# Transposing the Q and K rows in 32x32 blocks on VectorE instead of on TensorE

## The chip, the cores and the metric

The kernel runs on one core of one Trainium2 chip. The metric is the device time of that core in microseconds (us), as the median of several runs; lower is better.

## The reference

A two-layer model, each layer an attention with a recurrent memory (A) and a gated mixer (B), both with a residual. The change lies in A:

```python
# x: 2048 x 512, 32 heads of 128, memory of 8 tokens, segments of 32 tokens
for s in range(n_seg):                          # 64 segments, one after the other
    h = concat([mem, x[s]])                     # 8 + 32 = 40 tokens
    q, k, v = h @ Wq, h @ Wk, h @ Wv            # for every head
    scores = q @ k.T * scale                    # 40 x 40 for each head
    scores = where(mask, scores, -1e9)
    p = softmax(scores)
    o = (p @ v) @ Wo
    mem = o[:8]                                 # the next segment's memory
    outs.append(o[8:])
```

The model is x + A(layernorm(x)), then x + B(layernorm(x)), and both once more with the same weights. The memory makes the 64 segments of an attention block a chain. There are two attention blocks, 128 segments in all.

## The kernel before

Each attention block (a_block) works through 16 groups of 128 tokens, each of 4 segments. All weights stay in SBUF. A segment's 40 tokens are split: hA holds 32 of them (8 of memory, which come late, and 24 of x), and the other 8 come from hB, the last 8 tokens of each segment of the group, gathered in 32 rows. So the projections of 32 tokens use 32-wide weights in four column groups of TensorE (tile_position (0, 32*cg)), each group with another 512 columns of W.

In order, a segment does:

- psm (L545): Q and K of hA, four quarters (j = 0, 2, 1, 3; j < 2 is Q, else K) of 16 matmuls of 512 columns. ScalarE copies each to SBUF as rows (L548): tokens of four column groups on the partitions.
- emit_T (L512): four TensorE transposes for each quarter, into PSUM (pst), and a copy to KQ (L516 on ScalarE, L518 on VectorE), where the head dimension lies on the partitions. KQ holds 80 columns a head: K of 32 tokens, K of 8, Q of 32, Q of 8. The parts of 8 come from prep_segment (L491, L492 on POOL), which takes them from KTB and QTB.
- emit_S (L565): scores, a matmul for each head, 64-wide weights and 40 columns, in two halves. Then the exponentials: ETm for the memory's queries (L567), ETt for the others (L586), and the mask (L587).
- emit_V (L530): values, 64 matmuls in eight pieces of 8, laid between the steps above. They are evacuated to vs (L536 ScalarE, L538 VectorE).
- The row sums for the memory's queries (psD L579, reciprocal L582, spread with L589), PT (L592), psOm (L597), uT (L600), pw (L610, the product with Wo of the 8 memory rows), pw_sb (L613, L614), pmT (L626) and a reduction into the next segment's hA (L628). This is the recurrence.
- The same for the other 32 queries: row sums (L602, L605), psRt (L619), PT (L622), psOt (L633), copies into oT4 (L643).

Work that does not belong to the recurrence fills the time: fill(2) at four places of a segment takes two steps each from generators. gen_block_ln normalizes and transposes the next group; gen_bpass (L424 to L440) computes Q and K of that group's hB: psb, a copy to rowsB (L433), four TensorE transposes (pstB, L437), a copy to KTB or QTB (L440), in twelve steps; gen_y (L449) multiplies the finished group by Wo, in eight steps (psy). The order of the instructions on an engine follows the code, though a scheduler may move an instruction that is ready ahead of one that is not.

PSUM has two pools of four banks: acc (psm, pst, psv, psb, pstB, pw, pmT, psy, pT) and att (psS, psD, psOm, psRt, psOt). KQ comes from a pool of three buffers.

Of the kernel before, what the change touches and what calls it, by code (L numbers as in the profile page):

```python
# [14 lines left out]
P = 128  # L15
DM = 512
# [311 lines left out]
def a_block(tc, c, xd, MV_in, MV_out, mem0, wqkv, Wo, S):  # L328
# [8 lines left out]
    with ExitStack() as ctx:  # L337
# [12 lines left out]

        m0 = rowp.tile([M, DM], BF16, name="m0", tag="rowsQK", bufs=4)
        nc.sync.dma_start(m0[:], mem0.rearrange("b m d -> (b m) d"))
# [59 lines left out]
        def gen_bpass(tb):  # L412
            bs = blk_state[tb]
            hB = bs["hB"]
            KTB = blkp.tile([P, H, 32], BF16, name="KTB")
            QTB = blkp.tile([P, H, 32], BF16, name="QTB")
            bs.update(KTB=KTB, QTB=QTB)
            pend = []
            for j in (0, 2, 1, 3):
                psb = acc.tile([P, 512], F32, name="psb")  # L420
                for kt in range(KT):
                    for cg in range(4):
                        W_sb, col0 = wcat(chunk_of(j, cg))
                        nc.tensor.matmul(psb[32 * cg:32 * cg + 32, :], lhsT=hB[:, kt, :], rhs=W_sb[:, kt, col0:col0 + 512],  # L424
                                         start=(kt == 0), stop=(kt == KT - 1), tile_position=(0, 32 * cg))
# [5 lines left out]
                if True:  # L431
                    rB = rowp.tile([P, 512], BF16, name="rowsB", bufs=2)
                    nc.vector.tensor_copy(rB[:], psb[:])  # L433
                    yield
                    pstB = acc.tile([P, 4, P], BF16, name="pstB")
                    for hh in range(4):
                        nc.tensor.transpose(pstB[:, hh, :], rB[:, hh * P:(hh + 1) * P], ident_bf[:])  # L437
# [48 lines left out]
        def prep_segment(s):  # L486
            tb, j4 = s // 4, s % 4
            bs = blk_state[tb]
            KQ = kqp.tile([P, H, 80], BF16, name="KQ")
            vs = vsp.tile([P, 16, DH], BF16, name="vs")  # L490
            nc.gpsimd.tensor_copy(KQ[:, :, 32:40], bs["KTB"][:, :, 8 * j4:8 * j4 + 8])  # L491
            nc.gpsimd.tensor_copy(KQ[:, :, 72:80], bs["QTB"][:, :, 8 * j4:8 * j4 + 8])  # L492
            seg_state[s] = dict(KQ=KQ, vs=vs)

        def segment(s):
            tb, j4 = s // 4, s % 4
            st = seg_state.pop(s)
            KQ, vs = st["KQ"], st["vs"]
            KQf = KQ[:].rearrange("p h c -> p (h c)")
            hA_cur, hA_nxt = hA[s % NHA], hA[(s + 1) % NHA]  # L500
# [3 lines left out]
            rows = {}  # L504
            pst_tiles = {}

            def emit_T(ti, j):
                if ti % 2 == 0:
                    pst_tiles[ti // 2] = acc.tile([P, 2, 4, P], BF16, name="pst")
                pst = pst_tiles[ti // 2][:, ti % 2]  # L510
                for hh in range(4):
                    nc.tensor.transpose(pst[:, hh, :], rows[j][:, hh * P:(hh + 1) * P], ident_bf[:])  # L512
                src = pst.rearrange("p hh (g2 c2 r) -> p hh g2 c2 r", g2=2, c2=2)
                dst = heads_view(KQ[:, :, 40:72] if j < 2 else KQ[:, :, 0:32], j % 2)
                if ti % 2 == 0:
                    nc.scalar.copy(dst, src)  # L516
                else:
                    nc.vector.tensor_copy(dst, src)  # L518

            vstate = {}  # L520

            def emit_V(c, half):
                if half == 0:
                    vstate[c] = acc.tile([P, 512], F32, name="psv")
                psv = vstate[c]
                for kt in range(2 * half, 2 * half + 2):
                    for cg in range(4):
                        g = cg // 2
                        col0 = 2048 * g + 512 * c
                        nc.tensor.matmul(psv[32 * cg:32 * cg + 32, :], lhsT=(hA_cur if cg % 2 == 0 else hB_cur)[:, kt, :],  # L530
                                         rhs=Wv_sb[:, kt, col0:col0 + 512],
                                         start=(kt == 0), stop=(kt == KT - 1), tile_position=(0, 32 * cg))
                if half == 1:
                    dstv = vs[:, 4 * c:4 * c + 4, :].rearrange("p h e -> p (h e)")
                    if c % 2 == 0:
                        nc.scalar.copy(dstv, psv[:])  # L536
                    else:
                        nc.vector.tensor_copy(dstv, psv[:])  # L538

            for ji, j in enumerate((0, 2, 1, 3)):  # L540
                psm = acc.tile([P, 512], F32, name="psm")
                for kt in range(KT):
                    for cg in range(4):
                        W_sb, col0 = wcat(chunk_of(j, cg))
                        nc.tensor.matmul(psm[32 * cg:32 * cg + 32, :], lhsT=hA_cur[:, kt, :], rhs=W_sb[:, kt, col0:col0 + 512],  # L545
                                         start=(kt == 0), stop=(kt == KT - 1), tile_position=(0, 32 * cg))
                r = rowp.tile([P, 512], BF16, name="rows", tag="rowsQK", bufs=4)
                nc.scalar.copy(r[:], psm[:])  # L548
# [5 lines left out]
                if ji == 2:  # L554
                    emit_T(1, 2)
            psS = [att.tile([P, 8, 40], F32, name="psS") for _ in range(2)]
            ETm = segp.tile([P, 16, 8], BF16, name="ETm")
            ETt = segp.tile([P, 16, 32], BF16, name="ETt")

            def emit_S(half):  # L560
                for hl8 in range(8):
                    for g in range(2):
                        hl = 8 * half + hl8
                        h = 16 * g + hl
                        nc.tensor.matmul(psS[half][64 * g:64 * g + 64, hl8, :], lhsT=KQf[:, 80 * h:80 * h + 64], rhs=KQ[:, h, 40:80],  # L565
                                         start=True, stop=True, tile_position=(0, 64 * g))
                nc.scalar.activation(out=ETm[:, 8 * half:8 * half + 8, :], in_=psS[half][:, :, 0:8], func=ACT.Exp, scale=scale)  # L567
# [17 lines left out]
            for half in range(2):  # L585
                nc.scalar.activation(out=ETt[:, 8 * half:8 * half + 8, :], in_=psS[half][:, :, 8:40], func=ACT.Exp, scale=scale)  # L586
            nc.gpsimd.tensor_tensor(out=ETt[:], in0=ETt[:], in1=maskT[:].unsqueeze(1).to_broadcast([P, 16, 32]), op=ALU.mult)  # L587
            for g in range(2):
# [10 lines left out]
            for g in range(2):  # L599
                nc.scalar.copy(uT_cur[:, 16 * g:16 * g + 16, 0:8], psOm[g][:])  # L600
            for cq in range(4):
                nc.tensor.matmul(psD[:, 2 + 2 * cq:4 + 2 * cq], lhsT=ETt[:, 4 * cq:4 * cq + 4, :].rearrange("p h q -> p (h q)"),  # L602
                                 rhs=ind[:, 0:2], start=True, stop=True)
            with nc.allow_low_precision(reason="softmax 1/denominator stored in bf16 (probabilities are bf16 anyway)"):
                nc.vector.reciprocal(out=Rc[:, 2:10], in_=psD[:, 2:10])  # L605
            fill(FILLU)
            pw = acc.tile([P, 512], F32, name="pw")
# [6 lines left out]
            nc.vector.tensor_copy(pw_sb[:, 256:512], pw[:, 256:512])  # L614
            fill(FILLU)
            psRt = att.tile([P, 512], F32, name="psRt")
            for cq in range(4):
# [23 lines left out]
            oT4 = blk_state[tb]["oT4"]  # L641
            for g in range(2):
                nc.vector.tensor_copy(oT4[:, 16 * g:16 * g + 16, 32 * j4:32 * j4 + 32], psOt[g][:])  # L643
            fill(FILLU)
# [54 lines left out]
```

## Time and profile before

| | us |
|---|---|
| median of 3 runs | 2994.6 (2994.12 to 3000.23) |
| the profiled execution | 2987.32 |
| its span | 2985.4 |
| PE busy | 2670.5 (89%) |
| DVE busy | 1057.1 (35%) |
| ACT busy | 908.3 (30%) |
| POOL busy | 325.4 (11%) |
| mean granted TensorE clock | 0.977 |

PE is TensorE's matmuls, PEld its weight loads, DVE VectorE, ACT ScalarE, POOL GpSimd. The chain is the work that ended last, followed back from the last instruction; its shares say where the span went. An instruction's line number, such as L545, is its line in the kernel. x16 is the number of instructions in a row. Where matmuls overlap, their own durations (a few hundred ns) say less than the time that a run of them takes in the chain.

### The profile page before, as it was taken

The page shows a single profiled execution, that of the slowest core. Times are in us where ns is not written, and L with a number is a line of the kernel's source. Part 1 is how long each engine was busy: PE and PEld are TensorE (multiplying, and loading weights), DVE is VectorE, ACT ScalarE, POOL GpSimd, SP SyncE. Part 2 cuts the span into 40 slices and gives each one's busy share as a digit, 9 for nine tenths or more (in the row PEclk, how much of TensorE's full clock was granted, in tenths as well). Part 3 has the DMA queues.
Part 4 walks back from the last instruction along what each step waited for, and adds up shares of the span by engine and source line. Part 5 has one row for each costly group of instructions (what it writes and reads, how often), then busy time and mean ns, then how long its engine had stood idle before and what let it go on. Part 6 is the DMA issues. An engine that isn't in the chain of part 4 may idle for free.

```text
span 2985.4 us, 94041 instructions
## 1 busy us (share of the span) xinstructions
PE 2670.5 (89%) x43154; PEld 1324.3 (44%) x43272; DVE 1057.1 (35%) x2582; ACT 908.3 (30%) x2114; POOL 325.4 (11%) x531
## 2 busy tenths in 40 slices
PE   0999999999999999983779999999999999999889
PEld 0444444444444444441554444444444444444456
DVE  3333333333333333341233333333333333333422
ACT  0333333333333333343003333333333333333430
POOL 1101110011001111000221110101001111111012
PEclk9999999999999999996898999999999999999999
DMA  8000000000000000027750000000000000000234
GB/s 316 2 10 9 9 9 9 9 9 9 9 9 9 9 9 9 6 97 134 155 169 2 9 9 9 9 9 9 9 9 9 10 9 9 9 9 5 97 89 110
DMA packets 105613, 107.80 MB, mean 36 GB/s; under 512 B 69776, under 2 KB 79360, under 8 KB 102144
## 3 DMA queue, kind: packets, MB, share of 16 engines
q1 hardware_dynamic: 79520, 46.88, 6.9%
q10 hardware_dynamic: 21728, 30.78, 3.0%
q0 software_dynamic: 3968, 24.12, 2.1%
q8 instruction: 338, 5.54, 0.7%
q14 instruction: 59, 0.48, 0.1%
HBM read 66.11 MB, written 18.87 MB: 28 GB/s over the span
## 4 chain that ended last, share of the span: by engine, by line
PE 82%; DVE 8%; issue 4%; DMA 3%; ACT 3%; POOL 0%; ACTq 0%; DVEq 0%; POOLq 0%; SPq 0%
PE psv L530 19%; PE psm L545 17%; PE pw L610 8%; PE psy L449 7%; PE pg L195 6%; PE pst L512 6%; PE psb L424 4%; PE psS L565 3%; DVE rowsB L433 2%; PE psOm L597 2%; PE pstB L437 2%; DVE vs L538 2%; PE pmT L626 2%; PE psOt L633 1%; DMA xb<-in_A_x_dram 1%
## 5 line engine op out<-in xcount | busy, mean ns | idle before, releaser
L530 PE MATMUL psv<-Wv_sb,hA 128*32 128x512 bf16 x4096 | 606.5, 383 | 0.0
L530 PE MATMUL psv<-Wv_sb,hBs 128*32 128x512 bf16 x4096 | 606.5, 383 | 0.0
L548 ACT CAST rows<-psm 128x512 bf16<-128x512 f32 x512 | 300.1, 586 | 881.2 <-PE psm L545 879.1
L518 DVE COPY KQ<-pst 128x512 bf16<-128x512 bf16 x256 | 108.7, 425 | 658.4 <-ACT vs L536 348.5
L587 POOL TENSOR_TENSOR ETt<-ETt,maskT 128x512 bf16<-128x512 bf16 x128 | 148.1, 1157 | 1282.0 <-ACT ETt L586 1281.8
L545 PE MATMUL psm<-Wq_sb,hA 128*32 128x512 bf16 x4096 | 274.3, 389 | 9.7 <-DVE hA L628 6.8
L545 PEld LDWEIGHTS <-hA 128*32 128x32 bf16 x8192 | 185.7, 97 | 205.9 <-issue 25.2
L545 PE MATMUL psm<-Wk_sb,hA 128*32 128x512 bf16 x4096 | 272.5, 387 | 0.0
L610 PE MATMUL pw<-Wo_sb,uT 128*32 128x512 bf16 x4096 | 249.5, 380 | 4.7 <-ACT uT L600 0.3
L195 PE MATMUL pg<-wspT,z2n 128*128 128x256 bf16 (+1 forms) x1536 | 176.6, 277 | 76.7 <-issue 76.7
L449 PE MATMUL psy<-Wo_sb,oT 128*128 128x512 bf16 x932 | 231.7, 380 | 8.5 <-issue 4.8
L538 DVE CAST vs<-psv 128x512 bf16<-128x512 f32 x256 | 177.1, 692 | 171.4 <-PE psv L530 171.4
L512 PEld LDWEIGHTS <-rows 128*128 128x128 bf16 x2048 | 116.3, 98 | 221.1 <-ACT KQ L516 107.0
L512 PE MATMUL pst<-ident_bf,rows 128*128 128x128 bf16 x2048 | 203.8, 222 | 0.9 <-ACT KQ L516 0.8
L195 PEld LDWEIGHTS <-z2n 128*128 128x128 bf16 (+1 forms) x1536 | 151.2, 100 | 101.9 <-issue 84.2
L536 ACT CAST vs<-psv 128x512 bf16<-128x512 f32 x256 | 150.1, 586 | 144.2 <-PE psv L530 144.2
L530 PEld LDWEIGHTS <-hA 128*32 128x32 bf16 x4096 | 155.0, 95 | 70.4
L530 PEld LDWEIGHTS <-hBs 128*32 128x32 bf16 x4096 | 154.9, 95 | 58.1
L643 DVE CAST oT<-psOt 128x512 bf16<-128x512 f32 x256 | 166.6, 683 | 6.4 <-PE psOt L633 6.2
L516 ACT COPY KQ<-pst 128x512 bf16<-128x512 bf16 x256 | 150.8, 589 | 22.3 <-PE pst L512 22.3
L610 PEld LDWEIGHTS <-uT 128*32 128x32 bf16 x4096 | 106.4, 96 | 113.0 <-ACT uT L600 16.1
L622 DVE TENSOR_TENSOR PT<-ETt,psRt 128x512 bf16<-128x512 bf16 x128 | 87.8, 686 | 145.4 <-PE psRt L619 139.6
(106 smaller groups left out, 2684.7 us busy)
## 6 DMA issues: line engine op xcount, KB each, us to landing
xs<-xd SPq DMA_DIRECT2D x48, 256.0 KB, 2.8
xs<-xd ACTq DMA_DIRECT2D x48, 256.0 KB, 4.9
xd<-xo SPq DMA_DIRECT2D x32, 256.0 KB, 2.0
Wq_sb<-in_A_Wq_dram POOLq DMA_DIRECT2D x6, 1024.0 KB, 32.7
Wk_sb<-in_A_Wk_dram POOLq DMA_DIRECT2D x6, 1024.0 KB, 41.1
Wv_sb<-in_A_Wv_dram POOLq DMA_DIRECT2D x6, 1024.0 KB, 31.6
Wo_sb<-in_A_Wo_dram ACTq DMA_DIRECT2D x4, 1024.0 KB, 14.8
Wo_sb<-in_A_Wo_dram POOLq DMA_DIRECT2D x4, 1024.0 KB, 20.3
```

The lines of the kernel that those rows point to most:

```text
L195: nc.tensor.matmul(pg[0:fsz, :], lhsT=z2n[:, st_i, f0:f0 + fsz], rhs=wspT[:, st_i, :], start=(st_i == 0), stop=(st_i == NT - 1))
L449: nc.tensor.matmul(psy[:, :], lhsT=bs["oT4"][:, h, :], rhs=Wo_sb[:, h, :], start=(h == 0), stop=(h == H - 1))
L512: nc.tensor.transpose(pst[:, hh, :], rows[j][:, hh * P:(hh + 1) * P], ident_bf[:])
L516: nc.scalar.copy(dst, src)
L530: nc.tensor.matmul(psv[32 * cg:32 * cg + 32, :], lhsT=(hA_cur if cg % 2 == 0 else hB_cur)[:, kt, :], rhs=Wv_sb[:, kt, col0:col0 + 512], st ...
L536: nc.scalar.copy(dstv, psv[:])
L538: nc.vector.tensor_copy(dstv, psv[:])
L545: nc.tensor.matmul(psm[32 * cg:32 * cg + 32, :], lhsT=hA_cur[:, kt, :], rhs=W_sb[:, kt, col0:col0 + 512], start=(kt == 0), stop=(kt == KT ...
L548: nc.scalar.copy(r[:], psm[:])
L587: nc.gpsimd.tensor_tensor(out=ETt[:], in0=ETt[:], in1=maskT[:].unsqueeze(1).to_broadcast([P, 16, 32]), op=ALU.mult)
L610: nc.tensor.matmul(pw[32 * cg:32 * cg + 32, :], lhsT=uT_cur[:, h, :], rhs=Wo_sb[:, h, :], start=(h < 4), stop=(h >= H - 4), tile_position= ...
L643: nc.vector.tensor_copy(oT4[:, 16 * g:16 * g + 16, 32 * j4:32 * j4 + 32], psOt[g][:])
```

## The change

- Q and K rows are transposed by VectorE, in 32x32 blocks from SBUF to SBUF, one instruction of 128x512 for each quarter, in emit_T and in gen_bpass. The TensorE transposes and the copies from PSUM are gone.
- So that blocks suffice, the four column groups of psm and psb no longer hold different heads but different 32-element parts of the same heads: qk_rhs reads W in runs of 32 elements, 128 elements apart.
- KQ is replaced by rings of three buffers KK and QQ, cleared once in each attention block. They hold, for each head, 32 columns for the 32 tokens and 32 columns for the 8 tokens, 24 of them zero. Scores are two matmuls for each head, with 32-wide weights and 64 columns, in four column groups.
- All vs copies go to ScalarE; of the two oT4 copies, one goes to ScalarE; the mask goes from POOL to VectorE.
- The row sums of the 32 queries and their reciprocal move behind pw and its filling. The filling place ahead of pw is removed: three fill(2) a segment instead of four. gen_bpass has eight steps instead of twelve.
- rowsQK has three buffers instead of four.

```diff
-        kqp = ctx.enter_context(tc.tile_pool(name="a_kq", bufs=3))
...
-        def heads_view(ap3, s2):
-            return ap3.rearrange("p (g2 s2 c2 hh) r -> p s2 hh g2 c2 r", g2=2, s2=2, c2=2)[:, s2]
+        def qk_rhs(j, kt, cg):
+            W_sb = Wq_sb if j < 2 else Wk_sb
+            return W_sb[:, kt, :].rearrange("p (g2 s2 i eb el) -> p s2 eb g2 i el", g2=2, s2=2, i=8, eb=4)[:, j % 2, cg]
...
+        NKQ = 3
+        KKr = [pers.tile([P, 2, 2, 16, 32], BF16, name=f"KK{i}") for i in range(NKQ)]
+        QQr = [pers.tile([P, 2, 2, 16, 32], BF16, name=f"QQ{i}") for i in range(NKQ)]
+        for t in KKr + QQr:
+            nc.gpsimd.memset(t[:], 0.0)
...
-                        W_sb, col0 = wcat(chunk_of(j, cg))
-                        nc.tensor.matmul(psb[32 * cg:32 * cg + 32, :], lhsT=hB[:, kt, :], rhs=W_sb[:, kt, col0:col0 + 512],
+                        nc.tensor.matmul(psb[32 * cg:32 * cg + 32, :], lhsT=hB[:, kt, :], rhs=qk_rhs(j, kt, cg),
...
-                    rB = rowp.tile([P, 512], BF16, name="rowsB", bufs=2)
-                    nc.vector.tensor_copy(rB[:], psb[:])
-                    yield
-                    pstB = acc.tile([P, 4, P], BF16, name="pstB")
-                    for hh in range(4):
-                        nc.tensor.transpose(pstB[:, hh, :], rB[:, hh * P:(hh + 1) * P], ident_bf[:])
-                    src = pstB[:].rearrange("p hh (g2 c2 r) -> p hh g2 c2 r", g2=2, c2=2)
-                    dst = heads_view((QTB if j < 2 else KTB)[:], j % 2)
-                    pend.append(lambda dst=dst, src=src: nc.vector.tensor_copy(dst, src))
-                    yield
+                rB = rowp.tile([P, 512], BF16, name="rowsB", bufs=2)
+                nc.vector.tensor_copy(rB[:], psb[:])
+                dst = (QTB if j < 2 else KTB)[:, j % 2].rearrange("p a b -> p (a b)")
+                pend.append(lambda dst=dst, rB=rB: nc.vector.transpose(out=dst, in_=rB[:]))
+                yield
...
             def emit_T(ti, j):
-                if ti % 2 == 0:
-                    pst_tiles[ti // 2] = acc.tile([P, 2, 4, P], BF16, name="pst")
-                pst = pst_tiles[ti // 2][:, ti % 2]
-                for hh in range(4):
-                    nc.tensor.transpose(pst[:, hh, :], rows[j][:, hh * P:(hh + 1) * P], ident_bf[:])
-                src = pst.rearrange("p hh (g2 c2 r) -> p hh g2 c2 r", g2=2, c2=2)
-                dst = heads_view(KQ[:, :, 40:72] if j < 2 else KQ[:, :, 0:32], j % 2)
-                if ti % 2 == 0:
-                    nc.scalar.copy(dst, src)
-                else:
-                    nc.vector.tensor_copy(dst, src)
+                dst = (QQ if j < 2 else KK)[:, 0, j % 2].rearrange("p a b -> p (a b)")
+                nc.vector.transpose(out=dst, in_=rows[j][:])
...
-                    if c % 2 == 0:
-                        nc.scalar.copy(dstv, psv[:])
-                    else:
-                        nc.vector.tensor_copy(dstv, psv[:])
+                    nc.scalar.copy(dstv, psv[:])
...
-            psS = [att.tile([P, 8, 40], F32, name="psS") for _ in range(2)]
+            psS = [att.tile([P, 8, 64], F32, name="psS") for _ in range(2)]
...
-                        nc.tensor.matmul(psS[half][64 * g:64 * g + 64, hl8, :], lhsT=KQf[:, 80 * h:80 * h + 64], rhs=KQ[:, h, 40:80],
-                                         start=True, stop=True, tile_position=(0, 64 * g))
+                        for part in range(2):
+                            nc.tensor.matmul(psS[half][64 * g + 32 * part:64 * g + 32 * part + 32, hl8, :],
+                                             lhsT=KK[:, part, half, 8 * g + hl8, :], rhs=QQ[:, :, half, 8 * g + hl8, :],
+                                             start=True, stop=True, tile_position=(0, 64 * g + 32 * part))
...
-            nc.gpsimd.tensor_tensor(out=ETt[:], in0=ETt[:], in1=maskT[:].unsqueeze(1).to_broadcast([P, 16, 32]), op=ALU.mult)
+            nc.vector.tensor_tensor(out=ETt[:], in0=ETt[:], in1=maskT[:].unsqueeze(1).to_broadcast([P, 16, 32]), op=ALU.mult)
...
-            for cq in range(4):
-                nc.tensor.matmul(psD[:, 2 + 2 * cq:4 + 2 * cq], ...   # row sums L602, reciprocal L605
-            fill(FILLU)
             pw = acc.tile([P, 512], F32, name="pw")
...
             fill(FILLU)
+            for cq in range(4):
+                nc.tensor.matmul(psD[:, 2 + 2 * cq:4 + 2 * cq], ...   # row sums, reciprocal
             psRt = att.tile([P, 512], F32, name="psRt")
...
-            for g in range(2):
-                nc.vector.tensor_copy(oT4[:, 16 * g:16 * g + 16, 32 * j4:32 * j4 + 32], psOt[g][:])
+            nc.scalar.copy(oT4[:, 0:16, 32 * j4:32 * j4 + 32], psOt[0][:])
+            nc.vector.tensor_copy(oT4[:, 16:32, 32 * j4:32 * j4 + 32], psOt[1][:])
```

More of the change, by code (lines that the diff above doesn't have):

```diff
@@ L349, in a_block @@
         att = _Tagged(ps_pool, "att", 4)
-        m0 = rowp.tile([M, DM], BF16, name="m0", tag="rowsQK", bufs=4)
+        m0 = rowp.tile([M, DM], BF16, name="m0", tag="rowsQK", bufs=3)
         nc.sync.dma_start(m0[:], mem0.rearrange("b m d -> (b m) d"))
@@ L414, in gen_bpass @@
             hB = bs["hB"]
-            KTB = blkp.tile([P, H, 32], BF16, name="KTB")
-            QTB = blkp.tile([P, H, 32], BF16, name="QTB")
+            KTB = blkp.tile([P, 2, 16, 32], BF16, name="KTB")
+            QTB = blkp.tile([P, 2, 16, 32], BF16, name="QTB")
             bs.update(KTB=KTB, QTB=QTB)
@@ L488, in prep_segment @@
             bs = blk_state[tb]
[L489 removed]
+            KK, QQ = KKr[s % NKQ], QQr[s % NKQ]
             vs = vsp.tile([P, 16, DH], BF16, name="vs")
[L491 to L493 removed]
+            nc.gpsimd.tensor_copy(KK[:, 1, :, :, 0:8], bs["KTB"][:, :, :, 8 * j4:8 * j4 + 8])
+            nc.gpsimd.tensor_copy(QQ[:, 1, :, :, 0:8], bs["QTB"][:, :, :, 8 * j4:8 * j4 + 8])
+            seg_state[s] = dict(KK=KK, QQ=QQ, vs=vs)
         def segment(s):
@@ L543, in segment @@
                     for cg in range(4):
-                        W_sb, col0 = wcat(chunk_of(j, cg))
-                        nc.tensor.matmul(psm[32 * cg:32 * cg + 32, :], lhsT=hA_cur[:, kt, :], rhs=W_sb[:, kt, col0:col0 + 512],
+                        nc.tensor.matmul(psm[32 * cg:32 * cg + 32, :], lhsT=hA_cur[:, kt, :], rhs=qk_rhs(j, kt, cg),
                                          start=(kt == 0), stop=(kt == KT - 1), tile_position=(0, 32 * cg))
-                r = rowp.tile([P, 512], BF16, name="rows", tag="rowsQK", bufs=4)
+                r = rowp.tile([P, 512], BF16, name="rows", tag="rowsQK", bufs=3)
                 nc.scalar.copy(r[:], psm[:])
@@ L600, in segment @@
                 nc.scalar.copy(uT_cur[:, 16 * g:16 * g + 16, 0:8], psOm[g][:])
-            for cq in range(4):
[L602 to L605, printed above, removed]
-            fill(FILLU)
             pw = acc.tile([P, 512], F32, name="pw")
@@ L615, in segment @@
             fill(FILLU)
+            for cq in range(4):
+                nc.tensor.matmul(psD[:, 2 + 2 * cq:4 + 2 * cq], lhsT=ETt[:, 4 * cq:4 * cq + 4, :].rearrange("p h q -> p (h q)"),
+                                 rhs=ind[:, 0:2], start=True, stop=True)
+            with nc.allow_low_precision(reason="softmax 1/denominator stored in bf16 (probabilities are bf16 anyway)"):
+                nc.vector.reciprocal(out=Rc[:, 2:10], in_=psD[:, 2:10])
             psRt = att.tile([P, 512], F32, name="psRt")
```

5 lines of the change are left out of this document (1 added, 4 removed).

## The prediction

> **What bounds the kernel now.** I read the page first: the share of each engine and the chain of work that ended last.
>
> ```profile
> span 2985.4 us, 94041 instructions
> PE 2670.5 (89%) x43154; PEld 1324.3 (44%) x43272; DVE 1057.1 (35%) x2582; ACT 908.3 (30%) x2114; POOL 325.4 (11%) x531
> ...
> PE 82%; DVE 8%; issue 4%; DMA 3%; ACT 3%; POOL 0%; ACTq 0%; DVEq 0%; POOLq 0%; SPq 0%
> PE psv L530 19%; PE psm L545 17%; PE pw L610 8%; PE psy L449 7%; PE pg L195 6%; PE pst L512 6%; PE psb L424 4%; PE psS L565 3%; DVE rowsB L433 2%; PE psOm L597 2%; PE pstB L437 2%; DVE vs L538 2%; PE pmT L626 2%; PE psOt L633 1%; DMA xb<-in_A_x_dram 1%
> ```
>
> TensorE holds 82% of the chain. Three of the listed pieces are what the change removes (pst 6%, pstB 2%) or stands around it (the rowsB wait on VectorE, 2%). So the question is what stands in the tensor queue of one segment, and where that queue waits. Next I took the busy time in the four segments of one group of 128 tokens, and in the group:
>
> ```profile
> 616.47:638.41 21.94, 21.54 (x320) 9.87 (x323) 5.39 (x12) 6.27 (x15) 1.87 (x3) 1.00 0.01 2
> 638.41:658.59 20.18, 18.05 (x340) 8.59 (x343) 10.96 (x30) 6.27 (x15) 1.16 (x1) 1.00 0.08 28
> 658.59:676.94 18.35, 17.73 (x332) 8.51 (x331) 6.64 (x16) 6.27 (x15) 1.86 (x3) 1.00 0.01 3
> 676.94:693.23 16.29, 15.50 (x292) 7.38 (x292) 5.22 (x13) 6.28 (x15) 2.65 (x6) 1.00 0.01 2
> 616.47:693.23 76.76, 72.82 (x1278) 34.35 (x1281) 28.21 (x70) 25.09 (x60) 7.54 (x12) 1.00 0.03 9
> ```
>
> The columns are the stretch, its length, then busy time of PE, PEld, DVE, ACT, POOL, and the granted clock (1.00). TensorE is busy 72.8 of 76.8 us; VectorE and ScalarE a third each. Two attention blocks of 16 groups give 32 groups, 32 x 76.76 = 2456 us of the span; the rest (the mixer blocks and the start) the change leaves as it is. Last, the chain in order of time through the fourth segment, which carries no filling work:
>
> ```profile
> 676.94 1.91 PE psm L545 x32
> 678.85 0.33 PE pst L512 x4
> ...
> 681.46 0.36 PE psS L565 x16
> ...
> 682.70 0.75 PE psv L530 x9
> ...
> 683.78 0.76 PE psv L530 x10
> ...
> 685.98 0.98 PE psv L530 x16
> ...
> 687.73 0.70 DVE vs L538
> ...
> 688.48 0.30 PE psOm L597 x8
> ...
> 688.82 0.28 ACT uT L600
> ...
> 689.14 1.91 PE pw L610 x32
> ...
> 691.33 0.70 DVE PT L622
> ...
> 692.88 0.30 DVE hA L628
> ```
>
> The columns are start, length, and the piece. Up to the last psv the chain never leaves TensorE: what is taken out of that queue shortens the segment by its full length. Behind it the chain goes through evacuations.
>
> **The change part by part.** The sum is made against the profiled execution, 2987.3 us (span 2985.4), which is 7.3 us under the median of the runs, 2994.6.
>
> Segment transposes. Four groups of four leave TensorE in each segment, 4 x 0.33 = 1.32 us, all on the chain. In their place VectorE gets four 32x32-block transposes of 128x512. The trace has none; the nearest rows are
>
> ```profile
> L548 ACT CAST rows<-psm 128x512 bf16<-128x512 f32 x512 | 300.1, 586 | 881.2 <-PE psm L545 879.1
> L587 POOL TENSOR_TENSOR ETt<-ETt,maskT 128x512 bf16<-128x512 bf16 x128 | 148.1, 1157 | 1282.0 <-ACT ETt L586 1281.8
> L516 ACT COPY KQ<-pst 128x512 bf16<-128x512 bf16 x256 | 150.8, 589 | 22.3 <-PE pst L512 22.3
> L622 DVE TENSOR_TENSOR PT<-ETt,psRt 128x512 bf16<-128x512 bf16 x128 | 87.8, 686 | 145.4 <-PE psRt L619 139.6
> ```
>
> I take 0.69 us, the VectorE row of as many elements; the ends are 0.59 (ScalarE's copies) and 1.16 us (POOL's row). Whether it hides is a matter of place:
>
> ```profile
> 601.38 0.59 ACT L548 CAST rows<-psm 128x512 bf16<-128x512 f32 x1 [4.64 <-PE psm L545]
> ...
> 602.24 0.59 ACT L548 CAST rows<-psm 128x512 bf16<-128x512 f32 x1 [0.28 <-PE psm L545]
> ...
> 604.85 0.59 ACT L548 CAST rows<-psm 128x512 bf16<-128x512 f32 x1 [0.72 <-PE psm L545]
> ```
>
> That segment began at 600.2. Row block 2 is in SBUF 2.6 us after the start, its transpose is done at 3.3; the first scores come after 64 psm matmuls, 2 x 1.91 = 3.8 us. Slack 0.5 us. Row block 3 is there at 4.6, less the two transposes (0.66) that no longer stand ahead of its matmuls, so at 4.0 to 4.6; its transpose ends by 5.3, and the second scores follow 24 psv matmuls at about 5.8. Slack 0.5 again. So the transposes cost nothing; without this cover they cost what rival B says. Three row buffers instead of four do no harm by this clock: the fourth row copy begins after the first transpose has ended.
>
> The value matmuls between the transposes come in odd pieces: 9 in 0.75 and 10 in 0.76, where 16 take 0.98 (0.061 each). Four of them work side by side in column groups, so a piece of 9 needs three turns. The excess is 0.35 us (1.51 - 19 x 0.061); with the transposes gone I take back 0.30, between 0 and 0.35.
>
> Scores. Sixteen matmuls of 40 columns with 64-wide weights (0.36 us, 22.5 ns each) become 32 of 64 columns with 32-wide weights, in four column groups, twice a segment. Ends: 0.36 us (the four groups side by side take it all up) and 32 x 22.5 ns = 0.72. Small matmuls issued as weight and product pairs stand in
>
> ```profile
> 636.15 0.50 PE psOt L633 x32
> ```
>
> 32 in 0.50 us. These are the nearest in number and width (32 columns), so I take 0.50: +0.14 a half, +0.28 a segment.
>
> The front of a segment therefore loses 1.32 + 0.30 - 0.28 = 1.34 us, x 128 = 171 us.
>
> The group's own projections (gen_bpass) and their filling. Same view of the chain, second and third segment:
>
> ```profile
> 652.52 0.89 PE psb L424 x16
> ...
> 653.44 0.70 DVE rowsB L433
> ...
> 655.13 0.59 PE pmT L626 x4
> ...
> 656.26 1.28 DVE oT L643 x2
> 657.54 0.61 DVE rowsB L433
> ...
> 670.55 0.76 PE psb L424 x11
> ...
> 673.04 0.33 PE pstB L437 x4
> ...
> 673.91 0.36 PE psRt L619 x8
> ...
> 674.97 0.70 DVE rowsB L433
> ```
>
> Here TensorE fills the time with psb and then waits for its own filling: rowsB has to leave PSUM before pstB can run, and in the second segment rowsB stands behind 1.28 us of oT. Second segment, from 652.52 to the next psm at 658.59: 6.07 us. With the transposes on VectorE, what is left there for TensorE is 32 psb (1.9), psRt (0.36), pmT (0.59) and psOt (0.50): 3.4 us, and nothing in it waits for rowsB. I take 2.6 off, since that tail is longer than the chain through pw_sb, pmT and the reduction. Third segment: from the end of pw, where pstB starts at 673.04, to 676.94 is 3.9 us, plus 16 psb ahead of pw, of which 11 took 0.76 (about 1.3 with the rest); afterwards 1.9 + 0.36 + 0.59 + 0.5 = 3.35, plus 0.36 for uT and 0.3 for vs, both uncovered: 5.2 - 4.0 = 1.2 off. The first segment loses the cover of uT (one of the four filling places is removed, the one that stood before pw): +0.36, less 0.2 for vs; +0.15. The fourth has the evacuation of vs by ScalarE (0.59 by the row of the same shape) instead of VectorE (0.70): -0.1. What remains of filling places, six units a segment, still carries the shorter list (eight units of psy, four of normalization, eight of psb) within the group. A group gains 2.6 + 1.2 - 0.15 + 0.1 = 3.75, x 32 = 120 us. Lower end 1.5 a group, 48 us, if what is late next (the reduction hA, 0.30, behind PT, 0.70, in VectorE's queue) takes its place.
>
> Moved and shifted work. VectorE loses two KQ copies, two vs copies and one oT half, and gains four transposes and the mask (0.69 us at most, by PT's row; POOL's took 1.157 and nobody on the chain waited for it): at or below 28 of 77 us busy. ScalarE swaps two KQ copies (0.589) for two vs copies (0.586) and gains one oT half of that price: about 7 of some 14 us. None is near to being the bound; their price is nothing as long as TensorE's queue is the longest. The row sums L602 and their reciprocal move behind pw. Without cover that is a reciprocal and psRt ahead of PT in the fourth segment; against it, the pw_sb copies now stand ahead of PT in VectorE's queue, and the reduction can come up to 0.8 us earlier. I take 0 for both, with -0.8 and +0.3 as ends (32 segments: -26 to +10 us).
>
> Once for each attention block, POOL clears six ring buffers of twice the elements of uT's memset:
>
> ```profile
> L380 POOL MEMSET uT<- 128x1024 bf16 x2 | 1.9, 949 | 58.9 <-DMA xd<-xf 58.8
> ...
> 73.88 0.61 PE pstB L437 x4
> ```
>
> 6 x 1.9 = 11.4 us ahead of the memsets that the first normalization waits for; 0 to 11 a block. I take 10 in all. The first group's projections, which run alone, lose three waits of 0.70 + 0.61: 4 us a block, 8 in all.
>
> Strided weights. psm and psb now read W as 16 runs of 32 elements, 128 apart, instead of 512 in a row. No matmul of the trace does that. Nearest: ScalarE's KQ copy writes runs of 32 at a pitch of 80 in 589 ns, its rows copy of the same size 586 in a row. So I take nothing; rival A has the other end. The Trainium skill, "SBUF — State Buffer", section "Door 1: The DMA port swizzle", says that reads keep full bandwidth if they hit a 16-byte line at least twice; a run of 32 bf16 does. No run here shows it for TensorE.
>
> **Sum.** 171 + 120 + 8 - 10 = 289 us. 2987.3 - 289 = 2698; with the 7.3 us of the median, 2706.
>
> **Rivals.**
> A, the other side: the strided weight reads stretch psm and psb. They are 128 + 32 times 3.8 us (64 matmuls, 2 x 1.91), 608 us in all. If they become 48% longer, the gain is gone; at twice the length the kernel takes 2706 + 608 = 3314 us. For it: every one of these matmuls changes, four column groups now read interleaved runs. Against it: ScalarE's row above. 7%.
>
> B, VectorE's transposes are late. At POOL's 1.16 us each the second ends at 1.8 (row block 0 is there, 601.97) + 2 x 1.16 = 4.1, 0.3 us after the scores want it. The fourth then ends at 6.4, where the second scores, themselves 0.3 late, want it at 6.1: another 0.3. 0.6 x 128 = 77 us back, 2783. It decides from about (3.8 - 1.8) / 2 = 1.0 us each. Against it: VectorE is idle most of a front. 10%. The Trainium skill, "VectorE: DVE Perf Modes", section "The three transpose paths", gives 311 ns for 128x128; four times that is an estimate of 1.24 us, and the time by the same steps would be about 2800. The trace has no such transpose.
>
> C, the scores are dear. At 22.5 ns each and with no odd pieces saved: +0.44 and +0.30 a segment, 95 us, 2801. For it: the same instruction with the same issue. Against it: 15.6 ns in psOt. 15%. The Trainium skill, "TensorE: Matmul & The Clock Gate", section "Wait — 56ns, not 53.3ns?", has a floor of about 25 ns from start to start for small matmuls; by it a half takes 0.80 us, and the sum would be 2706 + 0.60 x 128 = 2783. The psOt row is under that floor, which speaks against it here.
>
> D, the waits of the tails come back under another name (1.5 instead of 3.75 a group): 2778. 10%.
>
> E, more is gained: scores at 0.36 (-36), the reduction 0.8 us earlier (-26), memsets hidden (-10): 2634 and less. 10%.
>
> **How the numbers follow.** The forecast, 2706, has 48%, and reaches from 2650 to 2760. The range of 8 in 10 takes in B, C and D and most of E: 2620 to 2850. Slower needs A beyond 48%: 6%. Within 0.2%, which is about what a measurement of this kernel can tell from no change: 1%. Faster: 93%.
>
> **What would show it.** Group windows of about 67.5 us instead of 76.8; no pst and pstB rows; psS 32 in about 0.50 us; psv pieces of whole fours; vector transposes near 0.69 us; psm still 32 in 1.91 us (1.91 growing is A). A wait of the psS weight loads on VectorE of more than 0.1 us a half is B. Chains through rowsB gone from the second and third segments; if a wait of pw on uT, or of psm on hA, grows by more than 0.5 us a segment, that is D. The prediction is wrong if psm is longer, or if the fronts, psm to last psv, take over 9.8 us instead of the 10.8 of before.

## The result, and the profile after

The changed kernel takes 2541.2 us (median of 12 runs, 2521.2 to 2548.6) against 2991.2 us before (15 runs; the three that the prediction had gave 2994.6): a ratio of 0.8495, 95% interval 0.8471 to 0.8518, 450 us less. The forecast was 2706 with a range of 2620 to 2850. The sign was right, the size was not: 289 us less were forecast. The profiled execution has a span of 2538.3 us. One run of all those below, of the kernel with 64-wide scores, came at a granted clock of 0.936 where its fellows had 0.976 to 0.982, and is left out.

The page after: span, engines, and the chain by engine and by line.

```profile
span 2538.3 us, 96292 instructions
...
PE 2259.8 (89%) x44720; PEld 1210.5 (48%) x44808; DVE 1162.4 (46%) x2582; ACT 985.5 (39%) x2242; POOL 201.0 (8%) x415
...
PE 76%; DVE 7%; ACT 6%; DMA 5%; issue 4%; POOL 1%; SPq 0%; ACTq 0%; POOLq 0%; DVEq 0%
PE psv L517 17%; PE psm L528 16%; PE pw L589 10%; PE psy L447 9%; PE pg L195 7%; PE psb L428 4%; ACT vs L522 3%; PE psS L549 3%; PE pmT L610 2%; DMA xs<-xd 2%; PE psRt L603 2%; DVE rowsB L436 1%; DMA xb<-in_A_x_dram 1%; PE psOm L582 1%; PE py L206 1%
```

TensorE is busy for the same 89% of a shorter span. pst and pstB are gone from the chain, and rowsB is down from 2% to 1%; new in this list are ScalarE's vs copy (3%), a load, xs from xd (2%), and psRt (2%).

The windows of one group, the third, fourth, first and second segment, then the whole (columns as before: stretch, length, PE, PEld, DVE, ACT, POOL, the granted clock, and last the share and GB/s of the DMA engines):

```profile
617.23:631.61 14.38, 13.89 (x339) 7.23 (x332) 8.67 (x17) 6.62 (x16) 0.70 (x2) 1.00 0.01 3
631.61:644.88 13.27, 12.78 (x307) 6.60 (x307) 6.59 (x14) 6.76 (x17) 1.53 (x5) 1.00 0.01 2
644.88:664.36 19.48, 19.14 (x341) 9.62 (x347) 5.96 (x12) 6.66 (x16) 0.74 (x2) 1.00 0.01 3
664.36:681.59 17.23, 14.72 (x347) 7.47 (x347) 10.26 (x28) 7.46 (x17) 0.00 (x0) 1.00 0.10 33
617.23:681.59 64.36, 60.53 (x1330) 30.93 (x1328) 31.48 (x69) 27.51 (x64) 2.97 (x8) 1.00 0.04 11
```

76.76 us have become 64.36. The granted clock is 1.00 in both. This group is a long one, since its second segment waits for a load (below): by the median, a group went from 76.7 to 63.0 us.

Call front what lies between the start of a segment's psm and the end of its last psv, and tail what follows up to the next psm. Added up from the records of the two traces, the 128 fronts are 326 us shorter and the 126 tails within the two attention blocks 114, of 447 us by which the span is shorter; all the rest differs by 7. The chain through the fourth segment (631.61 to 644.88) is the counterpart of the one the prediction shows:

```profile
631.61 3.64 PE psm L528 x64
635.25 0.26 PE psS L549 x32
635.50 1.31 PE psv L517 x24
636.82 0.28 PE psS L549 x32
637.10 0.87 PE psv L517 x16
637.97 0.11 PE psD L564
638.08 0.98 PE psv L517 x16
...
639.24 0.57 PE psv L517 x8
639.83 0.59 ACT vs L522
...
640.73 0.34 PE psRt L603 x8
...
641.08 1.94 PE pw L589 x32
643.04 0.38 ACT pw_sb L592
...
644.54 0.30 DVE hA L612
```

And the pieces of the same segment before that the prediction did not show:

```profile
679.18 0.98 PE psm L545 x16
...
680.49 0.98 PE psm L545 x16
681.83 0.55 PE psv L530 x8
...
684.90 0.97 PE psv L530 x13
...
687.13 0.57 PE psv L530 x8
```

This front took 10.77 us and takes 8.20 (631.61 to 639.81): 2.57 us, where 1.34 was forecast. The reader can add it up: the transposes 1.32; psm 3.87 (1.91 + 0.98 + 0.98) to 3.64, 0.23; psS 0.72 to 0.54, 0.18; psv 4.58 (0.55 + 0.75 + 0.76 + 0.97 + 0.98 + 0.57) to 3.73, 0.85.

At the start of an attention block two forecast terms meet, the memsets and the first group's projections, which run alone. Chain at the start of the first block, before and then after:

```profile
71.18 1.93 PE psb L424 x16
...
103.72 1.91 PE psm L545 x32
```

```profile
65.89 5.85 POOL KK L382 x3
...
79.00 3.50 PE psb L428 x32
...
97.84 3.64 PE psm L528 x64
```

From the first psb to the second segment's psm: 32.5 us before, 18.8 after. The ring memsets delay that psb by 7.8 us, in this block alone; in the second they end while a transfer of 13.6 us (xd from xo) is still under way. The projections, from that psb to the first psm, take 8 us less in the first block and 7 in the second.

### The profile page after: what moved, and what is told of

It is laid out like the page before. It is cut to its first block, busy times and chain, and to the rows that moved or that the text cites. A ratio compares the mean times of both kernels' runs of the same rounds, so it can differ in the third digit from the quotient of the medians.

```text
span 2538.3 us, 96292 instructions
## 1 busy us (share of the span) xinstructions
PE 2259.8 (89%) x44720; PEld 1210.5 (48%) x44808; DVE 1162.4 (46%) x2582; ACT 985.5 (39%) x2242; POOL 201.0 (8%) x415
## 4 chain that ended last, share of the span: by engine, by line
PE 76%; DVE 7%; ACT 6%; DMA 5%; issue 4%; POOL 1%; SPq 0%; ACTq 0%; POOLq 0%; DVEq 0%
PE psv L517 17%; PE psm L528 16%; PE pw L589 10%; PE psy L447 9%; PE pg L195 7%; PE psb L428 4%; ACT vs L522 3%; PE psS L549 3%; PE pmT L610 2%; DMA xs<-xd 2%; PE psRt L603 2%; DVE rowsB L436 1%; DMA xb<-in_A_x_dram 1%; PE psOm L582 1%; PE py L206 1%
## 5 line engine op out<-in xcount | busy, mean ns | idle before, releaser
L517 PE MATMUL psv<-Wv_sb,hBs 128*32 128x512 bf16 x4096 | 535.3, 381 | 0.0
L517 PE MATMUL psv<-Wv_sb,hA 128*32 128x512 bf16 x4096 | 534.7, 381 | 0.0
L522 ACT CAST vs<-psv 128x512 bf16<-128x512 f32 x512 | 299.6, 585 | 154.1 <-PE psv L517 137.2
L528 PEld LDWEIGHTS <-hA 128*32 128x32 bf16 x8192 | 209.9, 97 | 240.4 <-DVE hA L612 25.4
L528 PE MATMUL psm<-Wq_sb,hA 128*32 128x512 bf16 x4096 | 266.3, 380 | 18.8 <-DVE hA L612 18.8
L517 PEld LDWEIGHTS <-hA 128*32 128x32 bf16 x4096 | 180.5, 95 | 107.7
L505 DVE STREAM_TRANSPOSE QQ<-rows 128x512 bf16<-128x512 bf16 x256 | 181.4, 709 | 79.3 <-ACT rows L531 72.0
L626 ACT CAST oT<-psOt 128x512 bf16<-128x512 f32 x128 | 74.9, 585 | 365.2 <-PE psy L447 230.2
L505 DVE STREAM_TRANSPOSE KK<-rows 128x512 bf16<-128x512 bf16 x256 | 181.6, 709 | 29.3 <-ACT rows L531 24.7
L447 PEld LDWEIGHTS <-oT 128*128 128x128 bf16 x1024 | 95.1, 98 | 120.6 <-issue 12.7
L490 POOL COPY QQ<-QTB 128x256 bf16<-128x256 bf16 x128 | 49.6, 402 | 1272.2 <-DVE QTB L438 1222.1
L549 PEld LDWEIGHTS <-KK 128*32 128x32 bf16 x8192 | 89.7, 97 | 90.0 <-DVE KK L505 86.6
```

The source lines that it names most:

```text
L447: nc.tensor.matmul(psy[:, :], lhsT=bs["oT4"][:, h, :], rhs=Wo_sb[:, h, :], start=(h == 0), stop=(h == H - 1))
L505: nc.vector.transpose(out=dst, in_=rows[j][:])
L549: nc.tensor.matmul(psS[half][64 * g + 32 * part:64 * g + 32 * part + 32, hl8, :], lhsT=KK[:, part, half, 8 * g + hl8, :], rhs=QQ[:, :, hal ...
L626: nc.scalar.copy(oT4[:, 0:16, 32 * j4:32 * j4 + 32], psOt[0][:])
```

## The experiments

Theory M, formed on the trace after: what the forecast missed is the price of changing TensorE's tiling. A matmul whose weights are 128 or 64 wide, among matmuls with 32-wide weights in four column groups, costs about 0.11 us on the way in and again on the way out, besides its own work, as if the array ran empty each time. Before, a front changed eight times for transposes and four for 64-wide scores. The trace after carries the reading: 16 psv take 0.87 us behind psS, which is 32 wide, and 0.98 behind psD, which is not. Rival I: each instruction has its price. All changes below are against the changed kernel's 2541 us, and the ratios in brackets against the kernel before. The stretch between the two attention blocks, which these edits hardly touch, takes 247 to 282 us in the traces (270 in the one after the change); so the sums of fronts and tails from the traces are given beside the medians.

**A full-width matmul at four places, and its control.**

```diff
                 psm = acc.tile([P, 512], F32, name="psm")
+                if ji >= 2:
+                    nc.tensor.matmul(psm[:, 0:2], lhsT=ident_bf[:], rhs=ident_bf[:, 0:2], start=True, stop=True)
...
                     vstate[c] = acc.tile([P, 512], F32, name="psv")
+                    if c < 2:
+                        nc.tensor.matmul(vstate[c][:, 0:2], lhsT=ident_bf[:], rhs=ident_bf[:, 0:2], start=True, stop=True)
# control: the same, with
+  nc.tensor.matmul(psm[0:32, 0:2], lhsT=ident_bf[:, 0:32], rhs=ident_bf[:, 0:2], start=True, stop=True, tile_position=(0, 0))
```

> The changed kernel with one matmul of 2 columns and full 128-wide weights put in at four places of each segment: ahead of the third and fourth psm quarter and of the first two psv tiles. Its output is overwritten. Theory M: each place costs a change of the array's tiling forth and back, about 0.22 us, four a segment, 128 segments: 113 us slower (80 to 130). Rival (what cost time before was the transposes' own streaming, and a full-array matmul costs only its columns): under 10 us.

> The control to the run with a full-width matmul at four places: the same four places, 2 columns, but 32-wide weights in column group 0, the tiling that stands around it. Theory M: no change of tiling, at most a short turn of the array for each, 0.02 to 0.06 us, 10 to 30 us slower. If any inserted instruction costs the 0.22 us, it is as slow as the other, about 113 us.

Full width: 2631.6 us, 90 slower (ratio 0.8789, 0.8747 to 0.8831). Narrow: 2543.7, 3 slower (0.8507, 0.8473 to 0.8541). The chains, full width first (L529 and L513 are the inserted matmuls), then the control:

```profile
658.11 1.91 PE psm L532 x32
660.02 0.11 PE psm L529
660.13 0.98 PE psm L532 x16
...
661.21 0.98 PE psm L532 x16
```

```profile
648.50 3.66 PE psm L532 x61
```

One matmul of two columns stands 0.11 us in the chain and makes the 16 behind it take 0.98 instead of 0.87; psm goes from 3.64 to 4.09 us for two of them. The same instruction with 32-wide weights leaves 3.66. So it is not the instruction. Nor is it the width alone, by a row of the trace after:

```profile
656.64 3.19 PE psy L447 x14
```

psy has 128-wide weights behind 128-wide ones, and 512 columns take 0.228 us each there, about as much as a turn, four tiled matmuls of 512 columns side by side (0.87 / 4 = 0.218). The price of theory M is shown, at 0.22 us for a visit of another width. That the array runs empty meanwhile is a reading; no run here looks inside. The front grew by 0.83 us (658.11 to 667.14), which x 128 would be 106 us. The fronts of the whole trace are 92 us longer and the tails unchanged: the front of the second segment grew by 0.41 only, as it was waiting for something else (below).

**Scores 64 wide again.**

```diff
-                        for part in range(2):
-                            nc.tensor.matmul(psS[half][64 * g + 32 * part:64 * g + 32 * part + 32, hl8, :],
-                                             lhsT=KK[:, part, half, 8 * g + hl8, :], ..., tile_position=(0, 64 * g + 32 * part))
+                        i0 = min(8 * g + hl8, 14)
+                        nc.tensor.matmul(psS[half][64 * g:64 * g + 64, hl8, :],
+                                         lhsT=KK[:, 0, half, i0:i0 + 2, :].rearrange("p h c -> p (h c)"), ..., tile_position=(0, 64 * g))
```

> The changed kernel, but the scores are 16 matmuls a half with 64-wide weights in two column groups, as before the change, instead of 32 with 32-wide weights in four. The weights are two heads' K side by side, so the rows for the 8 late tokens hold other values; this is for time alone. Theory M (TensorE pays about 0.11 us whenever the width of the column tiles changes: a piece of 16 psv takes 0.87 us behind the 32-wide psS and 0.98 behind psD): psS then starts and ends with such a change, 0.26 grows to about 0.33 and the psv piece behind it by 0.11, 0.18 a half, 256 halves, 46 us slower (35 to 60). Theory I (a price for each instruction): half the matmuls, up to 0.13 a half less, 33 us faster.

2573.2 us, the median of three runs from 2564.5 to 2597.6, 32 slower (0.8618, 0.8558 to 0.8679). M said 46, and 35 to 60 as a range. The three runs are too far apart to tell these, but the fronts of the trace (of the run of 2597.6 us) are 45 us longer and its tails unchanged.

```profile
662.59 0.37 PE psS L549 x16
662.96 1.41 PE psv L517 x24
```

Half as many matmuls take 0.37 instead of 0.26 us, and the psv behind them 1.41 instead of 1.31. Rival I had this faster.

**Every score matmul twice.** `for part in range(2)` becomes `for part in (0, 1, 0, 1)`.

> The changed kernel with every score matmul issued twice (64 instead of 32 a half, same result). If four 32-wide matmuls stream side by side, a further four cost their 64 columns only, about 27 ns: +0.21 to 0.26 a half, 55 to 66 us slower. If each small matmul has a price of about 16 ns (the 0.50 us for 32 psOt on which the prediction rested): +0.5 a half, 131 us slower.

2632.4 us, 91 slower (0.8798, 0.8747 to 0.8850): between the two numbers. The chain of a half, and TensorE's waits (the trace is of a run of 2618.5 us):

```profile
663.68 0.51 PE psS L549 x47
```

```profile
PE psS L549 <- issue: 18.4, 18, 1.5
...
PE psv L517 <- issue: 12.3, 18, 1.2
```

32 further matmuls (the chain shows 47 of the 64) add 0.24 us a half, 7.5 ns each, 61 us in all. The 16 ns an instruction of the prediction is refuted for these matmuls. The fronts of this trace are 99 us longer in all; another 31 us of that are 18 pauses in the scores and 18 behind them, up to 1.5 us, for which the view shows no releaser, and some 8 are not assigned. The kernel after has no such pause. The trace's DMA records say what they are likely to be. The instruction queue q8 moves blocks of 16 KB, 414 here and 350 after the change: 64 more, for 16,384 more matmuls and weight loads. The records show 37 such pauses, 30.8 us, and each ends 1.2 to 1.6 us after a block has landed, though one lands only every 4.8 us (median). So TensorE most likely waited for its own instructions; no run took that cause away.

**The segment's transposes back on TensorE**, with W read in rows for psm; the new KK and QQ stay (the diff is shortened).

```diff
+                for hh in range(4):
+                    nc.tensor.transpose(pst[:, hh, :], rows[j][:, hh * P:(hh + 1) * P], ident_bf[:])
+                dst = (QQ if j < 2 else KK)[:, 0, j % 2].rearrange("p (g2 c2 hh) r -> p hh g2 c2 r", g2=2, c2=2)
+                (nc.scalar.copy if ti % 2 == 0 else nc.vector.tensor_copy)(dst, src)   # src: pst by head
-                nc.vector.transpose(out=dst, in_=rows[j][:])
```

> The changed kernel with the segment's transposes alone put back: psm reads W in rows of 512 and four groups of four TensorE transposes go to pst and from there to the new KK and QQ by ScalarE and VectorE, as before; all else is as changed. Theory M (transposes at 0.33, three pieces of psm instead of one, psv in odd pieces with a tiling change at each): 1.32 + 0.22 + 0.85 = 2.4 us a segment, 306 us slower. By the prediction's terms (1.32 + 0.30): 207 us slower.

2802.3 us, 261 slower (0.9370, 0.9335 to 0.9405), nearer to M's 306 than to the 207 of the prediction's terms.

```profile
672.96 0.33 PE pst L513 x4
...
675.83 0.45 PE psv L531 x8
676.27 0.33 PE pst L513 x4
676.60 0.75 PE psv L531 x9
677.35 0.33 PE pst L513 x4
677.68 0.76 PE psv L531 x10
```

The first psv piece, behind the 32-wide psS, takes 0.45 us for 8; the pieces behind transposes are 9 and 10 and take 0.75 and 0.76, three turns and a change of tiling (3 x 0.218 + 0.11 = 0.76). A front is 10.34 us here (634.12 to 644.46) against 8.20: 2.14, x 128 = 274; the fronts of the whole trace are 261 us longer, the tails unchanged. M's 306 held the changes around 64-wide scores too, which this run does not have. This one edit is more than half of the change's gain.

**The transposes of gen_bpass back on TensorE**, psb reading W in rows, with the filling place and the order of the row sums before the change, which its twelve steps need.

> The changed kernel with the transposes of gen_bpass put back on TensorE (twelve steps instead of eight), and with the row sums and the fourth filling place back ahead of pw, which the twelve steps need. By the prediction's tails 3.8 us a group, 32 groups, and the start: 100 to 130 us slower. If the waits on rowsB are covered now that VectorE has fewer copies from PSUM: the pstB groups alone, 4 x 0.4 us a group, 51 us slower.

2604.4 us, 63 slower than the changed kernel (0.8709, 0.8664 to 0.8753), but it holds the next experiment's order, which by itself is 26 us faster. Against that one it is 89 us slower. By the traces 81 us of this lie in the tails, 2.6 a group, and 8 at the start of the first block.

**The row sums and the filling place back ahead of pw.**

```diff
+            for cq in range(4):
+                nc.tensor.matmul(psD[:, 2 + 2 * cq:4 + 2 * cq], ...)
+            ... nc.vector.reciprocal(out=Rc[:, 2:10], in_=psD[:, 2:10])
+            fill(FILLU)
             pw = acc.tile([P, 512], F32, name="pw")
```

> The changed kernel with the row sums L602, their reciprocal and the filling place put back ahead of pw. The prediction put this move at nothing but the cover of uT (0.36 us in one or two of four segments): between 20 us faster and 10 slower. If the move is part of why the tails came out shorter: over 20 us slower.

2514.9 us, 26 faster (0.8412, 0.8380 to 0.8444), a little over the end of what was expected; the tails of its trace are 29 us shorter. The row sums themselves did not move: the changed kernel has them behind pw in its code, but its trace has them (L596) and psRt (L603) ahead of pw in all 128 segments, so the scheduler had put them there. What this run gives back is the filling place. TensorE's waits for the next group's tokens, after and in this run:

```profile
PE psb L428 <- DVE hB L414: 38.0, 30, 10.4
```

```profile
PE psb L428 <- DVE hB L414: 10.2, 2, 8.6
```

With the filling place gone, the next group's token transposes stand behind pw, and psb waits for nine VectorE copies out of them. With it, they stand between parts of psOm and are done under pw. Removing the filling place costs time.

**Copies and mask on their old engines** (vs by halves on VectorE, both oT4 copies on VectorE, the mask on POOL).

> The changed kernel with the copies and the mask where they were: two of four vs copies and both oT4 copies on VectorE, the mask on POOL. Expected: the last vs copy 0.70 instead of 0.59 ahead of psOm, 0.11 a segment, 14 us slower; if VectorE's longer queue makes the transposes late (its four take 0.71 each), 0.3 to 0.5 a segment more, 50 to 80 us slower.

2607.9 us, 67 slower (0.8715, 0.8676 to 0.8753). The number fell where late transposes were expected, but hardly for that reason: a front is 8.02 us long in this run (643.88 to 651.90) as after the change (617.23 to 625.25), and all fronts together are 10 us longer. It is the tails, 80 us longer together, while the stretch between the blocks is 23 shorter in this trace:

```profile
670.33 0.19 PE psRt L606
670.61 0.70 DVE PT L609
...
672.16 0.30 DVE hA L615
```

Here one psRt is left behind pw, PT follows it, and hA waits behind PT in VectorE's queue: 2.18 us from pw to the next psm, against 1.86 (643.02 to 644.88) after the change, where PT runs under pw. With 0.11 for vs, that is 0.43 us a segment, 55 of the 80 us; the rest lies in the second and third segments of the groups (their tails are 1.13 and 0.61 us longer) and is not assigned.

**W in rows again** (Q and K hold other columns).

> The changed kernel with psm and psb reading W in rows of 512 elements instead of 16 runs of 32; Q and K then hold other columns, so this is for time alone. The prediction's rival A (strided reads stretch these matmuls) would make it faster by what they are stretched; the trace has 64 psm in 3.64 us, 57 ns each, no longer than before. Expected: no difference, within 10 us.

2541.3 us, no difference (0.8498, 0.8457 to 0.8539). Runs of 32 elements cost TensorE nothing here.

**The next group's x earlier, and xn later.** The trace after shows a wait that the kernel before did not have (VectorE twice, then TensorE):

```profile
669.69 0.55 DVE L400 TENSOR_SCALAR xn<-xs,MV,rstd 128x512 bf16<-128x512 f32 x1 [1.28 <-DMA xs<-xd]
670.15 0.70 DVE L505 STREAM_TRANSPOSE KK<-rows 128x512 bf16<-128x512 bf16 x1
...
670.91 0.42 PE L549 MATMUL psS<-QQ,KK 128*32 128x64 bf16 x32 [1.45 <-DVE KK L505]
```

xn waits for a load, and the transpose that the scores need is queued behind xn.

```diff
# earlier load
-            xs = xp.tile([P, DM], F32, name="xs")
+            xs = xp.tile([P, DM], F32, name="xs", bufs=3)     # and NKQ = 2, for room
...
                 gens.append(gen_block_ln(tb + 1))
+                next(gens[-1])
# later xn: a second yield behind the load in gen_block_ln
```

> The changed kernel with the next group's x loaded a segment earlier, into a third buffer (the KK and QQ rings have two to make room). In the trace, the second segment of a group has VectorE waiting for that load with the transpose for the scores behind it in its queue: TensorE idles 1.45 us ahead of psS. Expected: 1.4 us a group, 32 groups, 45 us faster (25 to 60). If the wait is covered by something else: no difference.

> The changed kernel with the normalization xn of the next group one filling step later, so that it stands behind the transposes in VectorE's queue and not ahead of them; the load stays as it is. The same wait removed by another way: 45 us faster (25 to 60). If it is the load itself and not VectorE's order that holds the segment up: no difference.

Earlier load: 2520.1 us, 21 faster (0.8433, 0.8383 to 0.8482); less than expected, since only 14 groups wait. Its interval overlaps the changed kernel's a little; its trace no longer has the wait (0.2 us in all for psS on this transpose, 10.3 after). Its fronts are 15 us shorter and its tails 4; another 2 are gained at the start, where four rings are cleared and not six. Later xn: 2539.1, no difference (0.8491, 0.8451 to 0.8531), but the edit did not do what it was for: in its trace xn still stands ahead of that transpose (xn at 669.12, the transpose at 669.67, behind a load of 4.31 us). It tells nothing on the wait.

**Both faster edits together.**

> The changed kernel with the two edits that each made it faster: row sums and filling place back ahead of pw (26 us), and the next group's x loaded a segment earlier into a third buffer (21 us). If they remove different waits (psb on hB behind pw in the one, psS on the transpose behind xn in the other), they add: 2494 us (2485 to 2505). If one covers the other: 2510 to 2520.

2518.1 us (0.8417, 0.8392 to 0.8442): no faster than the order alone. The wait of psb on hB in this run:

```profile
PE psb L428 <- DVE hB L414: 24.3, 30, 6.9
```

The earlier load takes one filling step, so the steps behind it move up, and psb again follows its own token copies. One wait was exchanged for another: against the order alone, the fronts are 17 us shorter and the tails 23 longer. The best version is the changed kernel with its fourth filling place back: 2514.9 us.

## Why the prediction was wrong in size

The step that failed is the front of a segment, 1.34 us forecast, 2.57 measured. Three of its terms were mis-sized:

- Scores: +0.28 forecast, -0.18 measured, a miss of 0.46. The price of 16 ns for each matmul was taken from psOt, a row with 128-wide weights. In four column groups a matmul costs about 8 ns. The end that the prediction named and did not take, the four groups taking it all up, was too high as well.
- psv: 0.30 forecast, 0.85 measured, a miss of 0.55. The uneven pieces were seen; 0.35 was their size by the row of 16 in 0.98. That row itself held a change of tiling of 0.11, so the true turn was hidden in the yardstick.
- psm: nothing forecast, 0.23 measured: two changes of tiling fewer.

Together 1.24 us x 128 = 159 us. The fronts of the whole trace are 326 us shorter where 171 was forecast, a miss of 155, and 165 us lie between forecast and result. The terms were priced one at a time from rows that held a change of tiling, or left it out. The Trainium skill, "TensorEngine Tiling (Array Packing)", section "Key Properties", states that a change of tiling mode drains TensorE; it gives no price. The trace agrees, with 0.11 us on each side of the inserted matmul. The floor of 25 ns from the Trainium skill, "TensorE: Matmul & The Clock Gate", section "Wait — 56ns, not 53.3ns?", weighed in rival C, does not hold for matmuls in four column groups: 32 in 0.26 us.

What held: the transposes' 1.32 us. VectorE's transposes take 0.71 us (0.69 forecast),

```profile
L505 DVE STREAM_TRANSPOSE KK<-rows 128x512 bf16<-128x512 bf16 x256 | 181.6, 709 | 29.3 <-ACT rows L531 24.7
```

and are hidden in three of four segments. The tails gained 114 us in all, 3.6 a group, 3.75 forecast, but that the sum came so near is in part luck. From the first segment to the fourth they gained 0.0, 1.9, 1.3 and 0.5 us, where -0.15, 2.6, 1.2 and 0.1 were forecast. By the runs, gen_bpass is worth 2.6 a group; the copies and the mask on their new engines, put at nothing but some tenths for vs, are worth 2.5 (80 us); and the lost filling place takes 0.9 back (29 us). The memsets cost 7.8 us, 10 forecast; the projections that run alone gained 15 us in the two blocks, 8 forecast. Two sums of the prediction were off and did no harm. VectorE's busy time, put at or below 28 us a group, is 31.5: four transposes and the mask come to 3.45 us a segment by the prediction's prices, and the copies that leave VectorE to 2.9 by the rows before (two of 0.43, two of 0.69, one of 0.68). And rival B's time for transposes of 1.24 us each is 2829 us by its own steps (0.48 us late twice a segment), not about 2800. psm did not stretch: rival A is out, by the run with W in rows. C is out by the scores. B came in one place only, and not by the transposes' length: one of them stood behind xn. D came in part, as psb behind hB: the lost filling place, put at 0.15 us a group, cost 0.8. The move of the row sums, put at nothing, did not take place on the chip. E had the right sign and only a tenth of the chance: it took the scores' end at 0.36 and no tiling.

## What to carry to other kernels

Count in TensorE's queue how often the width of the weights changes among column-tiled matmuls, and price each visit of another width as a step of its own, beside its streaming; here a two-column matmul in the wrong tiling cost as much as four tiled matmuls of 512 columns side by side. Take a yardstick for a piece of work from a row without such a change in it. When filling steps are removed or merged, follow the engine queue behind each: the step that moves up can stand right behind its own producer, and one that waits for a load holds up what is queued behind it.

## What the runs showed that was not expected

- 0.22 us for a visit of a 128-wide matmul among 32-wide ones, and nothing measurable (3 us in 512 places) for a 32-wide one.
- About 8 ns for a matmul of 64 columns with 32-wide weights in four column groups, half of what the smallest matmuls cost before.
- Moving operands in runs of 32 bf16 at a pitch of 128 read at full rate (2541.3 against 2541.2 us).
- 32x32-block transposes of 128x512 bf16 on VectorE: 709 ns.
- Pauses in TensorE's queue, 31 us in all, in the kernel with the most matmuls, each ending 1.2 to 1.6 us after a 16 KB block of the instruction queue has landed.
- Instructions written behind pw ran ahead of it in every segment, so the code alone did not say what an edit of the order changed.
